# RWKV-5 attention and a balanced expert layer on one core: who copies a head in the opening, and the order of attention's first and last steps

## The chip, the cores and the metric

One NeuronCore of a Trainium2 chip. Its engines work side by side, each through its own queue in order: TensorE (PE; its weight loads are shown as PEld), VectorE (DVE), ScalarE (ACT), GpSimd (POOL), and SyncE (SP), which issues most DMAs. They wait for each other through semaphores. The metric is the device time of one execution in microseconds.

## What is computed

Float32 throughout. First a recurrent attention, batch 4, 8 heads, 768 steps, head size 48; then a router that gives each of the 3072 tokens to one of 8 experts, 384 tokens to each, by falling logit; then a two-layer network for each expert.

```python
for t in range(S):                                  # S = 768, D = 48
    kt, vt, rt = (k[:, :, t], v[:, :, t], r[:, :, t])
    cur = einsum('bhd,bhe->bhde', u * kt, vt)
    y[:, :, t] = einsum('bhd,bhde->bhe', rt, state + cur)
    state = w * state + einsum('bhd,bhe->bhde', kt, vt)
x = y as (3072, 384)
logits = x @ w_gate                                 # (3072, 8)
for idx in argsort(-logits.flatten()):              # give out tokens, 384 to an expert
    tok, e = idx // E, idx % E
    if assigned[tok] < 0 and counts[e] < cap: assigned[tok] = e; counts[e] += 1
for e in range(E):
    out[assigned == e] = maximum(x[assigned == e] @ w1[e], 0) @ w2[e]
```

## The kernel before

**Units.** Attention is cut into 24 units: 6 chunks of 128 time steps, and in each chunk the 4 batches, all 8 heads at once (`N` = 24, `B` = 4, `HP` = 4 pairs of heads). Unit n needs three loads of 192 KB each: k and r into one of five buffers `krs`, v into one of six `vts`. All are issued by SP in order, k, r, v; `load(n + 5, "kr")` and `load(n + 4, "v")` stand at the top of step n.

**The parts of a unit**, each a method of class `Mild`:

- `again(n)` (L338) copies one head of k and of r a second time within `krs`, so that pairs of heads can be taken in another pairing; one VectorE copy for both. `again_one(n, x)` (L342) does it for k (x = 0) or r (x = 1) alone, on ScalarE; before, the prologue uses it for units 0 to 2.
- `keys(n)` (L433): GpSimd multiplies k by a table of decay into `kss`. It needs the second copy of k's head.
- `own(n)` (L439): two GpSimd products into `rk`; `own_sum(n)` (L446): VectorE sums them into `dd`.
- `turn(n)` (L480): TensorE transposes kss (`kT_ps`) and r (`rT_ps`); ScalarE copies kT out, VectorE scales rT.
- `diagonal(n, zs)` (L486): eight ScalarE instructions fill the diagonals of `AT` from `dd`, four for each z.
- `pairs(n)` (L496), the products: eight TensorE matmuls into `g_ps`, then two VectorE mask copies (`COPY_PREDICATED`) into AT. There is one `g_ps`.
- `keep(n)` (L510), the state: TensorE's `kv_ps`, then VectorE and GpSimd update `states`.
- `outputs(n)` (L530): TensorE's `y_ps` from state and AT, then a ScalarE copy into x (L559).
- `rows(ns, tag)` (L600): TensorE transposes x (`x_ps`, L590), ScalarE copies it into `xr` (L597), SP stores it to `x_rows` in DRAM.
- `gate` (L563) and `logits` (L577), once a chunk: 16 matmuls into `lg_ps`, a ScalarE copy `lg`, a transpose and a copy into `LG`.
- `gate_weights` (L402), at n = 2: two DMAs issued from ScalarE's own queue.
- `idle(m, tag)` (L415): m transposes of the identity that nobody reads. `test` (L603): a small matmul and three VectorE steps that test the decay, at n = 12.

The order of all this is written out by hand: inside `tc.manual_schedule()` every engine gets its instructions in the order of the calls in `run` (L612). Step n mixes units: it turns unit n + 2, makes the products of n + 1, the outputs of n and the rows of n - 1. A buffer's wait comes from this order too. PSUM buffers are named by tag; `x_ps`, `lg_ps`, `lt_ps`, the test and the early search share the one called "few".

**The end of attention.** Behind it the search for the first expert's tokens is woven in. `early` (L1112) is a generator that VectorE and small TensorE matmuls (`e_cnt_ps`, `e_st_ps`, `e_some_ps`, `list_ps`) carry; the list `steps` says at which points of which step it is taken one stage further. After the last unit, `search` (matmuls `counts`, VectorE's `ind`, `own`, `cnt`, `wide`) looks for the next expert's threshold, and `go(m)` puts m matmuls of a first small expert block (`e_xT_ps`, `e_h_ps`, `e_o_ps`, generator `early` of the experts, L1674) between its stages. Then seven experts follow (`h_ps`, `p_ps`, `o_ps`).

The step before, without its head and its last lines:

```python
if n == 0:
    self.turn(2, True); self.again(3); self.own_sum(2); self.pairs(1); self.diagonal(2)
else:
    step(n, "first")
    if n + 3 < N: self.again(n + 3)
    if n + 2 < N:
        if n + 3 < N: self.own_sum(n + 2)
        self.turn(n + 2)
    if 1 < n <= N - B: self.rows((n - 1,), "few")
    if n + 2 < N: self.diagonal(n + 2)
    step(n, "turned")
    if n <= B: self.keep(n - 1)
    if n + 1 < N: self.pairs(n + 1, lambda: step(n, "products"))
    if n == 1: self.rows((0,), "few")
    step(n, "paired")
```

## Time and profile before

| what | us |
|---|---|
| four runs | 402.68, 402.73, 402.89, 406.03; median 402.81 |
| the profiled execution | 402.81, its span 401.1 |
| attention (to the last `y_ps`) | about 0 to 127 |
| first small expert block and search | about 131 to 159 |
| TensorE busy, 10 to 25 us | 10.75 of 15 |
| TensorE busy, 25 to 35 us | 10.00 of 10 |
| TensorE busy, 131 to 170 us | 36.02 of 39 |

In the profile a row of a timeline has the start, the time and the engine of a group of equal instructions, the source line, what is written and read, how many, and in brackets the idle time of the engine before it with what ended that. Waits of TensorE are listed by line and by what ended them. A loaded unit of k or r takes 4.2 to 4.6 us from issue to landing (median). The matmul ends are modelled, so that a small gap may be hidden in a busy row.

### The profile page before, as it was taken

The numbers are of one execution on the slowest core, as the hardware profiler recorded it, in microseconds if no ns is written. First come the engines' busy times: TensorE is split into PE (matmuls) and PEld (weight loads), VectorE is DVE, ScalarE is ACT, GpSimd is POOL, SyncE is SP. The second block draws the span as 40 slices with busy tenths as digits, with TensorE's granted clock in tenths as the row PEclk, the third lists the DMA queues.
The fourth block names the chain that finished last, engine by engine and source line by source line (L and its number), as shares of the span: only waits on it lengthen the run. The fifth ranks groups of instructions, "written<-read, shape, count | busy, mean of one in ns | idle before, by whom it ended". The sixth has DMA issues, their size and how long they took to land. (4 is left out here: it accounts for less than half of the span.)

```text
span 401.1 us, 8676 instructions
## 1 busy us (share of the span) xinstructions
PE 383.1 (96%) x3236; PEld 290.7 (72%) x3236; DVE 270.3 (67%) x939; ACT 160.8 (40%) x419; POOL 138.6 (35%) x173
## 2 busy tenths in 40 slices
PE   8789999999999899999999999999999999999993
PEld 6578888888877575578569558657756856966991
DVE  6676777576886787969649918969578762961630
ACT  4887878788873411222122221221222212222130
POOL 7787878566742022031120220301403212040020
PEclk9999999999999999999999999999999999999999
DMA  9999999888591264640290470107408274280010
GB/s 121 164 180 200 202 167 164 156 164 154 110 361 33 92 212 182 208 187 20 65 349 1 147 287 0 42 20 262 152 20 306 88 244 170 70 317 10 2 60 26
DMA packets 95331, 57.29 MB, mean 143 GB/s; under 512 B 77232, under 2 KB 89520, under 8 KB 95280
## 3 DMA queue, kind: packets, MB, share of 16 engines
q1 hardware_dynamic: 91520, 47.19, 47.5%
q0 software_dynamic: 3104, 9.44, 6.6%
q8 instruction: 27, 0.44, 0.5%
q14 instruction: 24, 0.20, 0.2%
q10 hardware_dynamic: 656, 0.01, 0.1%
HBM read 47.20 MB, written 9.44 MB: 141 GB/s over the span
## 5 line engine op out<-in xcount | busy, mean ns | idle before, releaser
L1518 PE MATMUL h_ps<-xT,w 128*128 128x384 f32 (+1 forms) x384 | 120.0, 466 | 0.0
L1518 PEld LDWEIGHTS h_ps<-xT,w 128*128 128x128 f32 x384 | 66.7, 190 | 38.6 <-issue 1.8
L1520 ACT ACTIVATE hid<-h_ps 128x384 f32<-128x384 f32 (+1 forms) x64 | 29.7, 464 | 90.4 <-PE h_ps L1518 84.6
L494 ACT ACTIVATE AT<-ident,dd 128x128 f32<-128x128 f32 x192 | 58.8, 391 | 3.2 <-DVE dd L448 3.2
L1614 POOL DMA_INDIRECT out_dram<-o_all,to x16 | 17.9, 1120 | 102.1 <-DVE o_all L1602 69.6
L1494 POOL DMA_INDIRECT xg<-x_rows,tok x22 | 22.5, 1021 | 85.3 <-issue 24.4
L507 DVE COPY_PREDICATED AT<-mask,g_ps 128x512 f32<-128x512 uint8 x48 | 32.6, 733 | 12.6 <-PE g_ps L503 12.3
L1597 ACT COPY res<-p_ps 128x384 f32<-128x384 f32 (+2 forms) x28 | 13.3, 474 | 60.5 <-PE p_ps L1593 58.4
L1620 PE MATMUL o_ps<-w,hid 128*128 128x384 f32 x96 | 33.2, 488 | 0.0
L503 PE MATMUL g_ps<-rT,kT 48*128 48x128 f32 x384 | 27.9, 285 | 0.6 <-DVE AT L507 0.6
L436 POOL TENSOR_TENSOR kss<-krs,wk 128x384 f32<-128x384 f32 x24 | 24.3, 1014 | 9.2 <-DVE krs L340 8.2
L503 PEld LDWEIGHTS g_ps<-rT,kT 48*128 48x128 f32 x384 | 23.3, 187 | 3.7 <-PE rT_ps L458 1.0
L541 PE MATMUL y_ps<-AT,vts 128*64 128x128 f32 x384 | 25.7, 276 | 0.0
L443 POOL TENSOR_TENSOR rk<-rk,u_bc 128x384 f32<-128x384 f32 x24 | 24.2, 1008 | 1.9
L442 POOL TENSOR_TENSOR rk<-krs 128x384 f32<-128x384 f32 x24 | 24.6, 1023 | 0.2 <-DMA krs<-in_r_dram 0.2
L1620 PEld LDWEIGHTS o_ps<-w,hid 128*128 128x128 f32 x96 | 17.2, 190 | 9.6 <-issue 0.3
L541 PEld LDWEIGHTS y_ps<-AT,vts 128*64 128x64 f32 x384 | 20.6, 137 | 1.0 <-issue 0.5
L1593 PE MATMUL p_ps<-T,S 128*128 128x192 f32 x120 | 20.9, 328 | 0.0
L1570 DVE TENSOR_TENSOR H<-hid 128x512 f32<-128x512 f32 x12 | 7.9, 686 | 19.1 <-ACT hid L1520 19.1
L559 ACT COPY x<-y_ps 128x512 f32<-128x512 f32 x24 | 14.0, 585 | 15.9 <-PE y_ps L541 15.9
L1593 PEld LDWEIGHTS p_ps<-T,S 128*128 128x128 f32 x120 | 19.6, 190 | 0.1
L477 DVE TENSOR_TENSOR rT<-rT_ps,WR 112x512 f32<-112x512 f32 x23 | 15.8, 686 | 4.7 <-PE rT_ps L458 4.6
(303 smaller groups left out, 690.0 us busy)
## 6 DMA issues: line engine op xcount, KB each, us to landing
w<-in_moe_w_dram SPq DMA_DIRECT2D x18, 1536.0 KB, 8.8
krs<-in_k_dram SPq DMA_DIRECT2D x24, 192.0 KB, 4.2
krs<-in_r_dram SPq DMA_DIRECT2D x24, 192.0 KB, 4.6
vts<-in_v_dram SPq DMA_DIRECT2D x24, 192.0 KB, 4.5
x_rows<-xr SPq DMA_DIRECT2D x24, 192.0 KB, 2.9
xg<-x_rows,tok POOLq DMA_INDIRECT x22, 4.7
out_dram<-o_all,to POOLq DMA_INDIRECT x16, 2.7
out_dram<-o_sb,to POOLq DMA_INDIRECT x5, 2.7
```

The source lines that it names most:

```text
L436: self.nc.gpsimd.tensor_mul(self.kss[:, n % self.NS].rearrange("p (g h) d -> p g h d", g=2)[:, :, :, 0:D], src, self.wk.rearrange("p (g h) ...
L442: nc.gpsimd.tensor_mul(rk, self.krs[:, n % self.NK, 1, 0:H, 0:D], self.krs[:, n % self.NK, 0, 0:H, 0:D])
L443: nc.gpsimd.tensor_mul(rk, rk, self.u_bc)
L494: nc.scalar.mul(AT[:, z, a, :], self.ident, dd[:, h:h + 1])
L503: nc.tensor.matmul(g_ps[:, z, a, :], kT[rows, a, :], rT[rows, a, :], start=True, stop=True)
L507: nc.vector.copy_predicated(out=AT[:, z], mask=self.mask.unsqueeze(1).to_broadcast([128, HP, T]), data=g_ps[:, z])
L541: nc.tensor.matmul(yv[q * PD:(q + 1) * PD, o // 2, o % 2, :], lhsT, rhs, start=(o // 2, q) not in seen, stop=stop, skip_group_check=True)
L1494: nc.gpsimd.indirect_dma_start(out=xg[:, c, :], out_offset=None, in_=x_dram[0:within, :], in_offset=bass.IndirectOffsetOnAxis(ap=tok[:, c: ...
L1518: nc.tensor.matmul(h_ps[:, 0:m], w1[:, f, ts(j, 128)], xT[:, f, 0:m], start=(f == 0), stop=(f == KD - 1))
L1520: nc.scalar.activation(hid[:, j, 0:m], h_ps[:, 0:m], AF.Relu)
L1593: nc.tensor.matmul(ps[:, q, :], left[a][:, j, :], right[b][:, j, :], start=(j == 0), stop=(j == KF // 2 - 1))
L1620: nc.tensor.matmul(o_ps, hid[:, j, ts(c, 128)], w2[:, j, :], start=(j == 0), stop=(j == KF - 1))
```

## The change

- **Opening, heads.** For units 3 to 7 (n = 0 to 4) the VectorE copy of a head of k and r is replaced by two ScalarE copies, k's before the diagonals of unit n + 2 and r's behind them (or behind their first half).
- **Opening, order.** At n = 1 and 2 the state of unit n - 1 and the products of unit n + 1 stand ahead of the turn of unit n + 2, and the diagonals of unit n + 2 are split around the outputs. `rows((0,))` moves behind the turn. At n = 0, `keys(1)` is called ahead of the heads of unit 3 and `keys(3)`; at n = 2 `own_sum` comes first.
- **Opening, unread transposes.** Two ahead of r0's transposes, two ahead of k1's, three ahead of the products of unit 1.
- **Middle.** `test` moves from n = 12 to n = 13.
- **Attention's last steps.** Two stages of the early search go later: `e_st_ps` from "turned" to "products" (n = 19), `e_some_ps` from "products" to "states" (n = 20). The row transposes of units 20 and 21 move from behind the last gate to ahead of the outputs of the last unit, with the search's last stages around them. The last gate is made in one group. The rows of the last unit go ahead of the small expert block's start, and the shares `go(m)` between the stages of the search change. The early expert's two results `e_o_ps` exchange their PSUM banks.

```diff
         k0 = self.keys_turned(0, True)
         self.again_one(0, 1)
+        self.idle(2, "g_ps")
         r0 = self.r_turned(0)
...
         self.again_one(1, 1)
+        self.idle(2, "g_ps")
         k1 = self.keys_turned(1, True, walk.ps, "few")
...
+            soon, split = n <= B, 0 < n < 3
+            halves = ((0,), (1,)) if split else ((0, 1), ())
             if n == 0:
                 self.turn(2, True)
-                self.again(3)
                 self.own_sum(2)
+                self.idle(3, "y_ps")
                 self.pairs(1)
-                self.diagonal(2)
+                self.keys(1)
             else:
                 step(n, "first")
-                if n + 3 < N:
+                if not soon and n + 3 < N:
                     self.again(n + 3)
+                if n == 2:
+                    self.own_sum(n + 2)
+                if split:
+                    self.keep(n - 1)
+                    self.pairs(n + 1)
                 if n + 2 < N:
-                    if n + 3 < N:
+                    if n != 2 and n + 3 < N:
                         self.own_sum(n + 2)
                     self.turn(n + 2)
-                if 1 < n <= N - B:
+                if n <= N - B:
                     self.rows((n - 1,), "few")
-                if n + 2 < N:
-                    self.diagonal(n + 2)
+            if soon:
+                self.again_one(n + 3, 0)
+            if n + 2 < N:
+                self.diagonal(n + 2, halves[0])
+            if soon:
+                self.again_one(n + 3, 1)
+            if n > 2:
                 step(n, "turned")
                 if n <= B:
                     self.keep(n - 1)
                 if n + 1 < N:
                     self.pairs(n + 1, lambda: step(n, "products"))
-                if n == 1:
-                    self.rows((0,), "few")
                 step(n, "paired")
...
-                if n < 2:
-                    self.keys(n + 1)
+                if n == 1:
+                    self.keys(2)
...
+            if n == N - 1:
+                self.rows((N - 4, N - 3), "g_ps")
+                step(n, "rows")
             self.outputs(n, lambda: step(n, "states"))
+            if split:
+                self.diagonal(n + 2, halves[1])
...
-            if n == N // 2:
+            if n == N // 2 + 1:
...
-        self.gate(C - 1, range(B - 1))
-        two = self.rows_turned((N - 4, N - 3), "g_ps")
-        self.gate(C - 1, [B - 1])
+        self.gate(C - 1, range(B))
         one = self.rows_turned((N - 2,), "kT_ps")
         self.logits(C - 1)
-        return two, one
+        return one, self.rows_turned((N - 1,), "g_ps")
...
-                o_ps = ps.tile([128, DX], F32, name="e_o_ps", tag=("y_ps", "g_ps")[c % 2])
+                o_ps = ps.tile([128, DX], F32, name="e_o_ps", tag=("g_ps", "y_ps")[c % 2])
...
-            steps = [(U - 7, "first"), (U - 7, "paired"), (U - 6, "paired"), (U - 5, "turned"), (U - 5, "paired"),
-                     (U - 4, "products"), (U - 3, "first"), (U - 3, "paired"), (U - 2, "last"),
-                     (U - 1, "states"), (U - 1, "last")]
+            steps = [(U - 7, "first"), (U - 7, "paired"), (U - 6, "paired"), (U - 5, "products"), (U - 5, "paired"),
+                     (U - 4, "states"), (U - 3, "first"), (U - 3, "paired"), (U - 2, "last"),
+                     (U - 1, "rows"), (U - 1, "last")]
...
+                mild.rows_out((U - 2,), one)
                 go(NE)
-                mild.rows_out((U - 4, U - 3), two)
-                mild.rows_out((U - 2,), one)
+                mild.rows_out((U - 1,), last)
...
-                for m in (0, 3, 2, 4, 2, 5, 6):
+                for m in (2, 5, 2, 5, 2, 6, 5):
                     next(search)
                     go(m)
-                    if not m:
-                        mild.rows((U - 1,), "g_ps")
...
-                go(8)
-                for m in (2, 4, 2, 99):
+                go(7)
+                for m in (2, 3, 1, 99):
```

## The prediction

> **What bounds the kernel now.** I read the busy line and the slices first, then TensorE's waits over the whole span, then ScalarE's timeline around 20 us.

> ```profile
> PE 383.1 (96%) x3236; PEld 290.7 (72%) x3236; DVE 270.3 (67%) x939; ACT 160.8 (40%) x419; POOL 138.6 (35%) x173
> ...
> PE   8789999999999899999999999999999999999993
> ...
> ACT  4887878788873411222122221221222212222130
> ```

> TensorE (PE) is the bound: from 170 us to 390 us its windows are full, so a microsecond gained or lost earlier is passed on to the end. What can be won lies in its gaps before 170 us:

> ```profile
> engine line waited for: us in total, times, longest us
> PE x_ps L590 <- ACT x L559: 1.6, 1, 1.6
> PE kT_ps L458 <- POOL kss L436: 1.5, 1, 1.5
> PE unread_ps L418 <- POOL ident masks.py:199: 1.4, 1, 1.4
> PE counts L925 <- DVE ind L913: 1.3, 2, 0.6
> PE g_ps L503 <- DVE AT L507: 0.6, 1, 0.6
> PE y_ps L541 <- ACT x L559: 0.6, 1, 0.6
> PE xT_ps L1509 <- ACT e_o_sb L1700: 0.6, 1, 0.6
> PE e_st_ps L1144 <- ACT xr L597: 0.6, 1, 0.6
> PE lg_ps L570 <- DVE e_some L913: 0.6, 1, 0.6
> ```

> The opening holds 4.25 us of them (0.54 at 12.6, 0.63 at 13.85, 1.50 at 17.53, 1.58 at 24.47); attention's last steps and the search after them hold the rest. Now ScalarE (ACT), in the place on which I think the opening turns:

> ```profile
> 21.93 0.33 ACTq L404 DMA_DIRECT2D wgp<-in_moe_w_gate_dram  x1
> 22.02 1.55 ACT L494 ACTIVATE AT<-ident,dd 128x128 f32<-128x128 f32 x5
> 23.48 0.46 ACT L597 COPY xr<-x_ps 128x384 f32<-128x384 f32 x1
> 23.83 0.58 ACT L559 COPY x<-y_ps 128x512 f32<-128x512 f32 x1
> 24.07 0.33 ACTq L404 DMA_DIRECT2D wgp<-in_moe_w_gate_dram  x1
> 24.44 0.59 ACT L475 COPY kT<-kT_ps 112x512 f32<-112x512 f32 x1
> ```

> The two gate-weight issues follow each other in the program, yet 2.14 us lie between them: in the built program each first waits for the completion that an older load reports on the same semaphore. The second goes out at 24.07; r of unit 5 landed at 24.05 (landing: the last of a load's sixteen completions in the trace). Here it cost nothing, because x was still being copied until 24.41.

> **The sum is made** against the profiled execution's 402.81 us (span 401.1 and 1.7 around it), which is also the median of the four runs.

> **Opening up to 24 us: gains.** r of unit 3 landed at 16.09, k at 14.89; VectorE's head copy of both (0.21) waits for r. Apart, k's copy frees GpSimd's kss 1.2 us sooner. kss of unit 1, put ahead, fits into GpSimd's idle 1.75 us before 16.47. I laid the rows in the new order: y of unit 0 ends at 16.04, then state (0.60), products of unit 2 at 16.7 (before: 19.15; VectorE no longer waits for r ahead of the mask copies), turn 3 at 17.8, y of unit 1 at 19.2 (20.78), products of unit 3 at 20.8 (25.60), turn 4 at 21.9, y of unit 2 at 23.3 against 26.69. So TensorE is 3.4 us ahead. The seven unread transposes cost nothing: four at 0.27 lie ahead of r0 and k1 and push g0 by 0.1, which the wait for r2 at 12.6 absorbs; three at 0.11 lie in the 0.63 gap, and would cost 0.33 without it.

> **Opening from 24 us: it is given back.** In the new build the two gate issues wait one load further on: for r5 (24.05) and v4 (25.19). Behind them in ScalarE's queue stand the kT copy of unit 4 (its transposes are done by 22.6), xr of unit 1 and the new head copy of k5; kss5, hence turn 5, hence TensorE wait for these. From 25.2: kT 0.49 and xr 0.39 start to start, head copy 0.22 to 26.35, GpSimd's kss 1.01 plus 0.08 to 27.45, turn 5 at 27.5 against 27.72. Of 3.4 us, 0.2 stays, and a gap of 3.1 us opens on TensorE. Then the head copies themselves: ScalarE was 4.71 and 4.79 us busy in the five-microsecond windows from 25 and 30 us; two copies a unit, 0.12 each start to start, make it run without a break. From 25.2 to the copy of x of unit 3 stand 16 diagonals (2.45 for eight), two kT, two xr, one x and four head copies: 4.8+1.0+0.8+0.5+0.5 = 7.5, so it starts at 32.7 (31.96 before), ends at 33.3, and its transposes, at 32.76 before, wait until then. Sum: **+0.5 us**. Bounds: k5 landed 2.06 us after v3 where its neighbours are 1.1 to 1.2 apart; without that dip everything here is 0.85 sooner, so -0.4 (ends -0.4 to +1.0). VectorE loses five copies of 0.2; only the one at 16.18, counted above, was on the path.

> [...]

> If ScalarE's later instructions pass a waiting issue, its 7.5 us start at 22.9, when the diagonals before them end, x of unit 3 ends at 31.0 instead of 33.3, and the opening gives -1.7. I take +0.5, as the copy of kT at 24.44 did not pass the issue of 24.07 either.

> [...]

> **Test one unit later.** The test's matmul at 77.79 waited 0.52 for the copy of the logits, with the same PSUM bank; turn 14 started at 77.81 where 77.10 was possible. In the next unit no logits are in that bank: **-0.7**. Its three VectorE steps (0.16 each) are hidden under products and row transposes, and would cost 0.5 without them.

> **Early search, moved by half a step.** Gone: e_st's wait (108.25 to 108.89, 0.6), since products go ahead, and lg's (0.56). New: e_st's VectorE steps (2.4 us from 109.12 to 111.56) start 1.3 us later against the products, so the mask copies behind them are late and the next products wait some 0.4 for their bank. And e_some now stands behind the gate matmuls, whose bank it takes: it waits for the lg copy, which stands on ScalarE behind eight diagonals. Before, that copy ended at 117.39, 3.8 us after products at 113.59; TensorE gets there 1.09+1.01+0.60 = 2.7 after them: a wait of 1.1, or 1.85 with VectorE's delay. Sum between -0.6-0.56+1.1 = -0.1 and -0.6-0.56+0.4+1.85 = +1.1; nearer to the upper, because the delay is a matter of order: **+0.9**.

> **Tail.** The eight row transposes (0.98) that stood at 128.34 go up into the 0.57 wait at 125.60: -0.6. The last unit's rows no longer wait for earlier row copies (0.44 at 133.36). Between two counts of the search VectorE needs 3.1 us (136.15 to 139.25); the new shares give TensorE 7 e_h matmuls of 0.43, 3.0 us, for each, so the 0.65 at 136.15 and some 0.2 go: -1.3. Sum **-1.9** (ends 0 and -2.6). The last gate in one group of 16 matmuls instead of 12 and 4, and the early expert's two results with their banks exchanged, are the same instructions: nothing, as long as the copy of the second result, for which 0.57 is waited at 158.8, does not come later. SP's queue is the same in both builds, so no load or row store passes another. The list of the second expert's tokens comes 1.8 us later, but its gather (issued from 147.48, median 4.7 to landing) had some 3.3 us in hand before the transposes at 158.8.

> Sum: 0.5 - 0.7 + 0.9 - 1.9 = -1.2, **401.6 us**.

> **Rivals.** (a) ScalarE is not held by the gate issues, or the loads land sooner: opening -1.7, sum -3.4, 399.4. For it: nothing in the trace shows the hold. Against: the 2.14 us. (b) Slower: the tail is paced by VectorE's search, not by TensorE. The waits for ind say so already (1.3 us in two); then filling TensorE's gaps with e_h matmuls only moves them ahead of the search, and the second expert's gather is what ends last. Price: the 1.9 us do not come, +0.7, 403.5. It decides if the token list is later by more than the 3.3 us in hand; I find 1.8. (c) The change does all it seems to: the 3.4 us stay, no new wait at e_some (-1.2 there): 402.81-3.4-0.7-1.2-1.9 = 395.6; it needs both the hold and ScalarE's 95% to be harmless. (d) TensorE falls back to its slow clock in the new 3.1 us gap; the longest gap of the trace after warming is 1.58 us, and the four transposes behind it still took 0.60, as later. Price unknown: nothing, or units of 4.1 us at up to twice their time until the clock is back, at most 4: 401.6 to 405.6.

> **Chances.** Forecast 0.50, (a) 0.22, (b) 0.16, (c) 0.07, (d) 0.05. The range 399.0 to 403.8 takes in the forecast with its bounds, (a) and (b). One per cent is 4.0 us, about what a measurement of this kernel can tell from no change: faster than 398.8 has (c) and an edge of (a), 0.10; slower than 406.8 an edge of (d), 0.03; the rest 0.87.

> **What would show it.** Right: turn 5 within 0.5 us of 27.5 after a gap of about 3 us, with the kT copy of unit 4 just after the second gate issue near 25.2; ScalarE without idle time from there to 33; no wait at the test; e_some waiting 1 to 2 us for ScalarE's lg copy; counts reached with less than 0.3 us of wait. Wrong: kT of unit 4 copied near 22.6, or waits for ind as long as before.

## The result, and the profile after

The changed kernel takes 405.02 us (median of 52 runs, 401.69 to 406.92) against 402.85 us (median of 78 runs, 402.63 to 407.56): a ratio of 1.0034, with a 95% interval of 1.0022 to 1.0045. That is within one per cent, as most of the chances had it, but on the other side of no change, and 1.2 us above the range. The profiled execution took 405.27 us, its span 403.5, so 2.4 us more than the profiled one of before.

The busy line and two of the slices, of the page of the changed kernel:

```profile
PE 384.2 (95%) x3243; PEld 293.2 (73%) x3243; DVE 267.2 (66%) x934; ACT 161.8 (40%) x429; POOL 137.9 (34%) x173
...
PE   7869999999989899999999999999999999999993
PEclk9997999999998999999999999999999999999998
```

The clock row was nines from end to end before. Now it has a 7 in the fourth slice (30 to 40 us) and an 8 in the thirteenth (121 to 131 us). TensorE's waits over the span say what stands ahead of these places (the columns as before: total, times, longest):

```profile
PE kT_ps L458 <- POOL kss L436: 3.4, 1, 3.4
PE e_some_ps L1195 <- ACT lg L575: 1.7, 1, 1.7
...
PE e_xT_ps L1697 <- DMA xg<-x_rows,e_tok: 1.1, 1, 1.1
```

The waits for the test, for e_st, for the search's `ind` and `wide` and for the rows of the last unit are gone. The wait of `e_xT`, the small expert block's first transposes, for their gather is new and stands in no sum of the prediction. Two other new ones are longer than all that the kernel had before. The first is the hold that was forecast; ScalarE's timeline of the changed kernel:

```profile
21.72 1.28 ACT L494 ACTIVATE AT<-ident,dd 128x128 f32<-128x128 f32 x4
23.90 1.52 ACTq L404 DMA_DIRECT2D wgp<-in_moe_w_gate_dram  x2
25.46 0.58 ACT L475 COPY kT<-kT_ps 112x512 f32<-112x512 f32 x1 [2.47 <-DMA vts<-in_v_dram]
```

ScalarE does nothing for 2.47 us, although the kT that it should copy has been in PSUM since 22.5. What ended its idle time is named as a load of v, for which no copy of kT has a use: it is the completion for which the second gate issue waited (the issues went out at 23.90 and 25.1; v of unit 4 landed at 25.07, r of unit 5, for which the first waited, at 23.88). Now TensorE behind it, same kernel:

```profile
23.21 1.09 PE L541 MATMUL y_ps<-AT,vts 128*64 128x128 f32 x16
27.70 0.65 PE L458 MATMUL kT_ps<-ident,kss 128*112 128x128 f32 x4 [3.40 <-POOL kss L436]
...
30.45 2.08 PE L503 MATMUL g_ps<-rT,kT 48*128 48x128 f32 x16
32.46 1.97 PE L541 MATMUL y_ps<-AT,vts 128*64 128x128 f32 x16
...
36.91 1.16 PE L503 MATMUL g_ps<-rT,kT 48*128 48x128 f32 x16
```

Turn 5 starts at 27.70, where 27.72 was its time before. But the same 16 products take 2.08 us at 30.45 and 1.16 at 36.91: between 28.69 and 35.52 the granted clock (full speed is 1.00) is 0.50. It falls a second time behind e_some, as the windows of this kernel from 119 us show (stretch, its length, busy time and instructions of PE, PEld, DVE, ACT and POOL, then the clock, DMA share and GB/s):

```profile
119.00:120.00 1.00, 0.20 (x6) 0.17 (x5) 0.00 (x0) 0.75 (x4) 0.92 (x2) 1.00 0.99 393
120.00:121.00 1.00, 1.00 (x18) 0.83 (x16) 0.86 (x3) 0.00 (x0) 0.14 (x1) 0.93 1.14 331
121.00:122.00 1.00, 1.00 (x7) 0.91 (x5) 0.08 (x1) 0.67 (x2) 0.00 (x0) 0.50 1.11 259
```

Half speed for 6.83 and for 3.41 us costs up to 3.41 + 1.71 = 5.1 us of TensorE's work. Without it the span would be about 398.4 us (an estimate that counts all of the 5.1), a gain of 2.7: the instructions are in a better order and run slower. The 54 executions for which a mean clock was recorded tell the same: ten at 0.992 or 0.993 took 401.69 to 402.72 us, six at 0.989 took 403.14 to 403.98, 23 at 0.984 or 0.985 took 404.59 to 405.55, and 15 at 0.980 or 0.981 took 405.72 to 406.92. In none was the clock 0.998, as in the profiled run of before.

Theory: the gate issues hold ScalarE, the hold makes the gap, and TensorE's idle time itself costs the clock; the same holds for the wait of e_some. Rivals: the loads make the gap, not the issues; the clock falls by chance; or the late work costs the time, and the clock does not matter.

### The profile page after: what moved, and what is told of

Read it like the earlier page. It is cut to its first block, busy times and chain, and to the rows that moved or that the text cites. A ratio compares the mean times of both kernels' runs of the same rounds, so it can differ in the third digit from the quotient of the medians.

```text
span 403.5 us, 8691 instructions
## 1 busy us (share of the span) xinstructions
PE 384.2 (95%) x3243; PEld 293.2 (73%) x3243; DVE 267.2 (66%) x934; ACT 161.8 (40%) x429; POOL 137.9 (34%) x173
## 5 line engine op out<-in xcount | busy, mean ns | idle before, releaser
L494 ACT ACTIVATE AT<-ident,dd 128x128 f32<-128x128 f32 x192 | 59.1, 392 | 2.1 <-DVE dd L448 1.9
L1509 POOL DMA_INDIRECT xg<-x_rows,tok x22 | 22.1, 1004 | 90.3 <-issue 38.3
L507 DVE COPY_PREDICATED AT<-mask,g_ps 128x512 f32<-128x512 uint8 x48 | 32.6, 732 | 14.6 <-PE g_ps L503 13.3
L503 PE MATMUL g_ps<-rT,kT 48*128 48x128 f32 x384 | 29.3, 294 | 0.7 <-DVE AT L507 0.7
L436 POOL TENSOR_TENSOR kss<-krs,wk 128x384 f32<-128x384 f32 x24 | 24.3, 1014 | 12.8 <-DVE krs L340 5.4
L503 PEld LDWEIGHTS g_ps<-rT,kT 48*128 48x128 f32 x384 | 24.7, 196 | 4.1 <-PE unread_ps L418 0.6
L541 PE MATMUL y_ps<-AT,vts 128*64 128x128 f32 x384 | 26.7, 283 | 0.0
L541 PEld LDWEIGHTS y_ps<-AT,vts 128*64 128x64 f32 x384 | 21.3, 141 | 1.2 <-issue 0.7
L559 ACT COPY x<-y_ps 128x512 f32<-128x512 f32 x24 | 14.0, 585 | 17.1 <-PE y_ps L541 17.1
```

The source lines that it names most:

```text
L436: self.nc.gpsimd.tensor_mul(self.kss[:, n % self.NS].rearrange("p (g h) d -> p g h d", g=2)[:, :, :, 0:D], src, self.wk.rearrange("p (g h) ...
L494: nc.scalar.mul(AT[:, z, a, :], self.ident, dd[:, h:h + 1])
L503: nc.tensor.matmul(g_ps[:, z, a, :], kT[rows, a, :], rT[rows, a, :], start=True, stop=True)
L507: nc.vector.copy_predicated(out=AT[:, z], mask=self.mask.unsqueeze(1).to_broadcast([128, HP, T]), data=g_ps[:, z])
L541: nc.tensor.matmul(yv[q * PD:(q + 1) * PD, o // 2, o % 2, :], lhsT, rhs, start=(o // 2, q) not in seen, stop=stop, skip_group_check=True)
L1509: nc.gpsimd.indirect_dma_start(out=xg[:, c, :], out_offset=None, in_=x_dram[0:within, :], in_offset=bass.IndirectOffsetOnAxis(ap=tok[:, c: ...
```

## The experiments

**1. The gate issues on another queue.** SyncE issues them one unit earlier.

```diff
-            self.nc.scalar.dma_start(self.wgp[...
+            self.nc.sync.dma_start(self.wgp[...
...
-            if n == 2:
+            if n == 1:
                 self.gate_weights()
```

> The changed kernel, with the two gate-weight DMAs issued from SyncE's queue one unit earlier instead of from ScalarE's. Theory (the wait of these issues holds ScalarE, the 3.4 us gap of TensorE follows, and the gap costs the clock): ScalarE copies kT of unit 4 before 23.5 us instead of at 25.46, turn 5 starts before 26.5 instead of at 27.70, TensorE has no wait over 1.6 us between 10 and 35 us, the granted clock stays 1.00 from 10 to 110 us, and the first gate matmuls start before 34.5 instead of at 38.0. The drop behind e_some stays. Time: 405.0 - 3.4 (clock) - 2.2 (hold) = 399.4 us, 398.5 to 402. Rival 1 (loads, not the issues, hold unit 5): turn 5 stays within 0.5 of 27.7 and the time within 1 us of 405. Rival 2 (the clock falls by the chance of its phase, gap or not): turn 5 comes early, but the clock of the runs stays spread over 0.98 to 0.99 and the time falls by 2.2 only, 402.8.

400.29 us (398.30 to 400.50), ratio 0.9907 (0.9871 to 0.9943). ScalarE's and TensorE's timelines of this run:

```profile
22.02 1.28 ACT L494 ACTIVATE AT<-ident,dd 128x128 f32<-128x128 f32 x4
23.20 0.56 ACT L475 COPY kT<-kT_ps 112x512 f32<-112x512 f32 x1
```

```profile
25.44 0.65 PE L458 MATMUL kT_ps<-ident,kss 128*112 128x128 f32 x4 [0.81 <-POOL kss L436]
```

The copy of kT now follows the diagonals without a pause, 2.26 us sooner, turn 5 starts at 25.44 and the first gate matmuls at 33.45. The 16 products take 1.16 us at 27.72 and at 32.35, so nothing ran at half speed there, and the profiled execution has a mean clock of 0.993, where the changed kernel's has 0.984. The wait of e_some (1.7 us) is still there, and 0.993 against the 0.997 of run 3, which lacks it, leaves some 3 us of half speed for it (an estimate: 0.004 of 398.5 us, twice). Rival 1 is out: turn 5 starts 2.26 us sooner, and the heads of k and r of unit 5 are copied from 24.04 and 25.35 on, both before the 25.46 at which ScalarE goes on in the changed kernel. Rival 2 is out for the opening: with its gap, the low clock has gone too. The run changes two things, the queue and the place in it (a unit earlier); which of them was needed is not parted. Its run of 398.30 us has a mean clock of 0.997, so there the wait of e_some seems to have cost no clock.

**2. e_some back at the products.**

```diff
-                     (U - 4, "states"), (U - 3, "first"), ...
+                     (U - 4, "products"), (U - 3, "first"), ...
```

> The changed kernel, with only the stage e_some of the early search put back from the states to the products of its unit. Theory: its wait of 1.70 us for the logits' copy is gone (at most 0.3 left), the gate matmuls wait some 0.6 for VectorE's e_some again, and the granted clock stays 1.00 from 110 to 131 us. The opening stays as it is, with its gap of 3.4 us and its low clock. Time: 405.0 - 1.7 + 0.6 - 1.7 (clock) = 402.2 us, 401.3 to 403.2. Rival (the clock falls there whatever the wait, or by chance): the wait goes, the low clock near 121 us stays, 403.9 us.

403.10 us (400.25 to 404.75), ratio 0.9975 (0.9946 to 1.0004). The wait of 1.70 has gone, and that it takes its low clock with it is read from run 3, which differs only in the queue and the place of the gate issues and has a mean clock of 0.997; the gate matmuls wait 1.19 us for VectorE's e_some, twice what was expected. The opening kept its gap (3.0 us here), and the profiled execution has a mean clock of 0.983: against the 0.997 of run 3 that is some 11 us of half clock (an estimate: 0.014 of 401.9 us, twice), more than the 6.83 us of the changed kernel's opening. The time is inside its range (401.3 to 403.2), at its upper end. The runs follow their clock again: those at 0.983 took 403.7 to 404.8, the one at 0.996 took 400.25.

**3. Both edits.**

> Both edits together: gate-weight DMAs on SyncE's queue a unit earlier, e_some back at the products. Theory: no gap over 1.6 us on TensorE between 10 and 131 us, granted clock 1.00 from 10 us to the end but for the last few us, and the savings add: 405.0 - 5.6 - 2.8 = 396.6 us, 395.8 to 399.5, faster than the kernel before by over 3 us. Rival (only one of the two, or chance, decides the clock): no better than the better of the two alone, 399.4 or more.

397.99 us (397.94 to 398.04), ratio 0.9864 (0.9840 to 0.9888), the clock 0.997 or 0.998 in every run. The savings add, 1.4 us short of what was expected: the hold was taken at 2.2 us and is worth 1.4 (at the second gate the units are 1.77 us ahead of before, and those of the changed kernel, clock apart, some 0.35), and the gate matmuls wait 1.19 us for e_some instead of 0.6.

**4. The gap left, but filled.** This one parts the idle time from the late work.

```diff
+                    if n == 3:
+                        self.idle(28, "g_ps")
                     self.turn(n + 2)
```

> The changed kernel, with 28 more transposes of the identity that nobody reads on TensorE ahead of turn 5, as long together as its gap (about 3.1 us); all else as in the changed kernel, ScalarE held as before. Theory (an idle TensorE costs the clock, not the late work by itself): turn 5 stays at 27.7 within 0.4, the granted clock stays 1.00 from 10 to 110 us, time 405.0 - 3.4 = 401.6 us, 400.8 to 402.8. [...] Rival 2 (the low clock costs nothing, the held work does): the clock stays up and the time does not move.

402.68 us (401.14 to 403.15), ratio 0.9962 (0.9938 to 0.9985). TensorE's timeline of this run, and a window over one stretch in it:

```profile
25.53 3.25 PE L418 MATMUL unread_ps<-ident 128*128 128x128 f32 x28 [1.02 <-DVE AT L507]
28.61 0.60 PE L458 MATMUL kT_ps<-ident,kss 128*112 128x128 f32 x4
...
30.57 1.16 PE L503 MATMUL g_ps<-rT,kT 48*128 48x128 f32 x16
```

```profile
26.19:29.61 3.42, 3.42 (x34) 3.42 (x33) 0.00 (x0) 3.42 (x13) 2.81 (x3) 1.00 1.25 208
```

The filler waited 1.0 us for its bank, so turn 5 came at 28.61, 0.9 us later than in the changed kernel, where at most 0.4 was expected; and yet the kernel is 2.3 us faster, since the products behind it take 1.16 us and not 2.08. Here the idle time costs the clock, and late work alone does not; rival 2 is out, since the time moved although the work came later. From 26.19 to 29.61 TensorE did nothing but transposes, and the clock stayed at 1.00. The wait of e_some (1.7 us) is still there; the profiled execution's mean clock of 0.992, beside the 0.993 of run 1 with the same wait, leaves some 4 us of half speed for it (an estimate: 0.005 below the 0.997 of run 3, times 401.4 us, twice).

**5. The kernel before, its two longest waits filled.**

```diff
+                    if n == 1:
+                        self.idle(12, "kT_ps")
                     self.turn(n + 2)
+                if n == 2:
+                    self.idle(10, "g_ps")
```

> The kernel before, with 12 unread transposes ahead of turn 3 and 10 ahead of the rows of unit 1, in the places of its two waits of 1.50 and 1.58 us. Theory (the clock is set by how busy TensorE was in a stretch of 3.41 us that starts at any phase; its runs of 404 to 406 us with a mean clock of 0.986 to 0.990 are those in which a whole gap fell into one stretch): the mean clock of every run is 0.996 or more, and the times lie within 0.6 us of each other, 402.5 to 403.3. Rival (the spread of the kernel before has another cause): the clock of about half of the runs stays at 0.993 or less and times of 404 us and more stay.

403.27 us (403.03 to 403.89), while the kernel before on the same chip had a median of 404.27 and went from 402.70 to 406.26: ratio 0.9967 (0.9944 to 0.9991). The fillers put turn 5 0.5 us late, and still the spread shrinks from 3.6 to 0.9 us. The expectation failed in part: the times lie 0.9 us apart and not 0.6, and of the ten runs only three reach the mean clock of 0.996, four have 0.995 and three 0.986 to 0.990; the profiled run, at 0.997, does not show where it fell. No run took 404 us or more, as the rival would have it. A low mean does not always cost time: one of the three took 403.21 us, and the kernel before has runs of 402.94 us at 0.990 and 403.02 us at 0.986. Why is open. So most of the spread of the kernel before comes from these two waits; that it comes through the clock is seen in one execution, that of run 6.

**6. The last steps and the test alone,** on the kernel before, with e_some at the products. The diff is that of the change, from `test` on, without its line for e_some.

> The kernel before with only the middle and the end of the change: the test a unit later, e_st half a step later (e_some left at the products), the row transposes, the last gate and the shares of the small expert block as changed. Theory (parts add, each as in the runs with both waits gone): test -0.7, early search -0.6 + 0.6 = 0, tail -2.8, some 0.5 given back among the experts: 402.8 - 3.0 = 399.8 us, 399.0 to 400.6. Rival (VectorE's search paces the tail, the gain came from the opening alone): 401.9 or more.

400.02 us (399.57 to 401.18), ratio 0.9900 (0.9872 to 0.9929), inside the range expected: the rival in which VectorE's search paces the tail is out. This kernel has the opening of before, and its profiled run caught what that opening can cost (TensorE's timeline, then the windows over two stretches):

```profile
24.40 0.60 PE L590 MATMUL x_ps<-ident,x 112*128 112x112 f32 x4 [1.58 <-ACT x L559]
...
26.76 1.97 PE L541 MATMUL y_ps<-AT,vts 128*64 128x128 f32 x16
```

```profile
23.02:26.43 3.41, 2.03 (x36) 1.84 (x36) 1.85 (x5) 3.24 (x10) 3.21 (x4) 1.00 1.13 176
26.44:29.84 3.40, 3.40 (x28) 2.85 (x25) 1.94 (x4) 2.01 (x6) 2.64 (x4) 0.50 1.19 215
```

It is the wait of 1.58 us that the profile of before shows at 24.47 without harm. There it was cut in two by the edge of a stretch at 23.79 (an estimate: that trace's clock falls at 399.26, 110 times 3.413 us later; the last section has this distance), and the stretches on both sides were busy for 2.51 and 2.74 us; here most of it fell into one, which was busy for 2.03 of 3.41 us, and the next ran at a clock of 0.50.

**7. The opening alone,** with the gate issues on SyncE's queue, as in run 1.

> The kernel before with only the opening of the change, and the gate-weight DMAs on SyncE's queue at n = 1. Theory: turn 5 at 25.2 to 25.5 instead of 27.72, first gate matmuls at 33.2 to 33.5 instead of 34.93, and the 1.5 to 1.8 us stay to the end: 402.8 - 1.7 = 401.1 us, 400.5 to 401.9, the clock at 0.995 or more in most runs since no gap over 1 us is left in the opening. Rival (ScalarE's added copies give all of it back further on): 402.5 or more.

401.18 us (400.80 to 401.91), ratio 0.9939 (0.9920 to 0.9959). Turn 5 at 25.06, the first gate at 33.09, the second at 52.54 (54.39 before): 1.85 us stay for good, and the rival is out. Some 0.8 us of the 2.7 at turn 5 are given back by the first gate; that the ten added copies on ScalarE do it is likely, but no run leaves them out alone.

**8. e_some in a bank of its own,** where the change has it, with the issues as in run 1.

```diff
-            some_ps = ps.tile([128, Q, NE * Q], F32, name="e_some_ps", tag="few")
+            some_ps = ps.tile([128, Q, NE * Q], F32, name="e_some_ps", tag="counts")
```

> The kernel with the issues on SyncE's queue, e_some where the change has it (behind the gate matmuls), but in the PSUM bank of kv_ps and counts, which is free by then, instead of the one shared with lg_ps. Theory (the wait of 1.70 us is for the bank, not for data): e_some waits less than 0.3 us and the gate matmuls no longer wait 1.2 us for it as in the run with both edits: 398.0 - 1.2 = 396.8 us, 396.2 to 397.6, clock 0.996 or more. Rival (the next wait stands right behind: the copy of the logits or VectorE's row and value steps): 397.8 or more.

397.32 us (397.25 to 397.48), ratio 0.9835 (0.9791 to 0.9880), the clock 0.995 to 0.997. TensorE's timeline:

```profile
111.82 1.08 PE L570 MATMUL lg_ps<-x,wgp 128*32 128x128 f32 x32
112.83 0.67 PE L541 MATMUL y_ps<-rT,states 48*64 48x128 f32 x16
113.43 0.27 PE L1195 MATMUL e_some_ps<-e_vals,e_row 128*128 128x32 f16 x4
```

Three groups without a wait where the changed kernel lost 1.70 us and run 3 lost 1.19. The wait was for the bank. 0.49 of it comes back at `lt_ps`, which does need the logits' copy.

**9 and 10. Without the seven unread transposes, and run 8 again on the same chip.**

```diff
-        self.idle(2, "g_ps")
         r0 = self.r_turned(0)
...
-        self.idle(2, "g_ps")
         k1 = self.keys_turned(1, True, walk.ps, "few")
...
-                self.idle(3, "y_ps")
                 self.pairs(1)
```

> The kernel with the issues on SyncE's queue and e_some in its own bank, without the seven unread transposes that the change adds in the opening. Theory (they cost nothing and bring nothing, as forecast): within 0.3 us of the same kernel with them, 397.0 to 397.7. Rival 1 (they warm the clock one or two stretches of 3.41 us sooner, and that reaches the end): 0.4 to 1.5 us slower, 397.7 to 398.8. Rival 2 (they are in the way): 0.4 us or more faster, 396.9 or less.

> The kernel with the issues on SyncE's queue and e_some in the bank of kv_ps and counts once more, on the same chip as the one without the seven unread transposes. Theory: 397.3 us again, 396.9 to 397.7, all runs within 0.4 us of each other, 1.2% or more faster than the kernel before. Rival (the earlier four runs were lucky in their phase): runs over 398.5 appear, with a mean clock below 0.993.

397.41 us (397.06 to 399.25) without them and 397.51 (397.39 to 397.93) with them; against the kernel before 0.9830 (0.9797 to 0.9864) and 0.9836 (0.9802 to 0.9870). Run 10 spreads by 0.54 us, where 0.4 was expected, and none of its runs is over 398.5. The version of run 8 is thus 1.6% faster than the kernel before, and the transposes are not needed for it: with them and without, the medians lie 0.1 us apart. The one run of 399.25, at a mean clock of 0.990, is the profiled one. Its clock is 1.00 from 10 to 35 us, and in the tail it has a wait of 1.0 us of e_xT for its gather, where run 8 has 0.3. Against the 0.995 of run 10's profiled execution it ran some 4 us more at half speed (an estimate: 0.005 of 397.5 us, twice); that this was behind that wait is likely, but not shown. So this version is not quite safe from the clock either.

## Why the prediction was wrong

- **Hold and gap: right.** Forecast: kT of unit 4 copied behind the second gate issue near 25.2, turn 5 at 27.5 after a gap of 3.1. Measured: 25.46, 27.70, 3.40. Run 1 showed the cause. Of the two readings the trace of before left open, ScalarE's later instructions did wait behind a waiting issue here, as the sum had it: for 2.47 us.
- **The price of the gap: the step that failed.** The sum booked the gap as time alone: "Of 3.4 us, 0.2 stays, and a gap of 3.1 us opens on TensorE." The clock stood in rival (d) at 0.05, "401.6 to 405.6", on the ground that a gap of 1.58 us had done no harm in the one trace. That trace was lucky in its phase, as run 6 shows (the stretch with most of the gap busy for 60%; 74 and 80% on the two sides of the edge before). Measured: 6.83 us at half clock behind the gap, up to 3.4 us of TensorE's work, and no such loss when the gap was filled (run 4) or gone (runs 1 and 3). A hint was on record: one of the four runs of before took 406.03 us, and this spread went unread.
- **e_some: its wait right, its price not.** Forecast 1.1 to 1.85 us, measured 1.70. It cost the clock as well (1.7 us), which no case of the prediction had. The early search as a whole, clock apart: the kernels of runs 1 and 3 differ in this line alone. From the fourth gate to the first expert's matmuls run 1 needs 158.08 - 92.10 = 65.98 us, 64.27 without the 1.71 of the clock (taken as in the changed kernel), and run 3 needs 155.80 - 91.82 = 63.98. Run 3 takes as long as the kernel before from the fourth gate to the fifth (21.23 and 21.20 us). So about +0.3, forecast +0.9: mis-sized.
- **ScalarE after the hold: mis-sized.** Forecast +0.5 for the opening. At the second gate the changed kernel is 3.06 us late, up to 3.41 of it by the clock, which leaves about -0.3, near the lower bound of -0.4. (The five terms of its list behind 25.2 us add up to 7.6 us, not 7.5, which changes little.)
- **Test: right.** From the third gate to the fourth 20.47 us before and 19.74 after: -0.73, forecast -0.7.
- **Tail: mis-sized, inside its bounds.** From the fifth gate to the 101st matmul of the experts run 3 needs 109.31 us and the kernel before 111.74: -2.4, forecast -1.9 (0 to -2.6). Both waits for `ind` went in full, and so did that for `wide` (0.4), which the sum had left out; the new wait of `e_xT` for its gather, left out too, took back 0.5 in run 3 (1.1 in the changed kernel).
- **Unread transposes: right,** no cost (runs 9 and 10).
- **Rivals.** (a) and (c) needed a ScalarE that is not held. Run 1 made it so: 400.29 us, some 1.7 of them by estimate for the clock behind e_some, so about 398.6 against the 399.4 of (a). (b) fell with run 6. (d) was the case, inside its price; the second fall, behind e_some, it did not have.

Without the clock the changed kernel's steps come to 398.4 + 1.7 = 400.1 us, against 401.6 forecast: the working was 1.5 us too careful on the steps and had no 5.1 us for the clock.

## What to carry to other kernels

Work that is moved ahead has to be followed to the next thing that waits, and a gap on TensorE can have two prices: its time, and the half-speed work behind it, which here cost as much again (a gap of 3.40 us, and up to 3.41 us for the clock). Here two DMA issues that waited in ScalarE's queue held all that stood behind them, for 2.47 us; on SyncE's queue, a unit earlier, they cost nothing that shows. A spread of one per cent in a kernel's runs is worth reading beside their clocks before one run's gaps are taken as harmless.

## What the runs showed of the hardware

```profile
25.28:28.69 3.41, 0.99 (x9) 1.00 (x10) 0.55 (x1) 3.23 (x11) 1.98 (x3) 1.00 1.20 195
28.69:32.10 3.41, 3.41 (x35) 3.04 (x35) 1.42 (x3) 3.41 (x12) 2.54 (x3) 0.50 1.11 217
```

Of the full-speed stretches, laid out every 3.413 us from these edges, in the traces of the kernel before and of the changed one, and the one shown of run 6, three with matmuls in them were followed by a clock of 0.50: in the changed kernel those busy for 29% (25.28) and 50% (117.44), in run 6 the one busy for 60% (23.02). Two with as little kept the clock: 54% in the changed kernel (from 134.51 to 137.92, with the wait of 1.08 us of e_xT in it), and 52% in the kernel before (from 392.43 to 395.85, where its last matmul ends). All others in these two traces that held matmuls were busy for 64% or more, and behind none of them did the clock fall. The busy time is modelled, and the two kinds overlap from 52 to 60%, so no edge sharper than that is shown.

Waits of 1.58 us (run 6) and 1.70 us (the changed kernel) were enough here: behind both the clock was 0.50. A stretch of nothing but float32 transposes kept the clock: in run 4, from 26.19 to 29.61, TensorE was busy for 3.42 of 3.42 us at a clock of 1.00, and the products behind it, at 30.57, took 1.16 us. In the kernel before, after an opening made mostly of transposes, those into kT_ps took 421 ns each up to 8.4 us and 273 ns from 11.4 on.

How long the low clock lasts stays open. One full stretch brought it back behind e_some in the changed kernel (120.85 to 124.27) and in run 6 (26.44 to 29.84, with the transposes at 30.14 back at 0.55 us); two were needed in the changed kernel's opening (28.69 to 35.52), although TensorE was busy in the first for 3.41 of 3.41 us by the records. No run tells why.
